# A streaming scale-and-add: rows regrouped from two halves into three contiguous blocks of HBM

## The chip, the core and the metric

One core of one Trainium2 chip at a time. The metric is the device time of one execution in microseconds (us). All runs quoted were in the fast state; the granted clock was 1.0 in every one. Ratios are the mean time of one kernel's fast runs over the mean of the other's in the same rounds, with a 95% interval, so they are not quite the ratios of the medians quoted beside them.

## The reference

```python
B, S, D = 1024, 16, 512          # bf16
def reference(x, y, gamma):      # x, y: B x S x D; gamma: D
    return x + gamma * y
```

That is 16384 rows of 1 KB in each of x, y and the output, 128 rows for each of 128 partitions: 33.6 MB to read, 16.8 MB to write, and one multiply and one add for each element.

## The kernel before

The kernel is written on bare queues and semaphores. SP issues the loads, ACT issues the small gamma load and the stores, VectorE multiplies and adds in place in `y_sb`. Four lists say everything about the order: `SP` and `ACT` list transfers as (tensor, first row, last row, place in the x buffer), `PIECES` cuts a partition's 128 rows into VectorE's pieces, `DVE` is VectorE's order of multiplies and adds.

```python
PIECES = [53, 11, 53, 11]
SP = [('y', 0, 64), ('x', 0, 64, 0), ('y', 64, 128), ('x', 64, 117, 0), ('x', 117, 128, 64)]
ACT = [('g',), ('s', 0, 64), ('s', 64, 128)]
RELEASE = ('x', 64, 117, 0)
DVE = [('m', 0), ('m', 1), ('a', 0), ('a', 1), ('m', 2), ('m', 3), ('a', 2), ('a', 3)]
...
xv = xf.rearrange("(p n) d -> p n d", p=P)       # partition p owns rows 128p .. 128p+127
y_sb = nc.alloc_sbuf_tensor("y_sb", [P, rows, D], dt).ap()
x_sb = nc.alloc_sbuf_tensor("x_sb", [P, x_rows, D], dt).ap()   # x_rows = 75: reused
...
            if need > known:
                eng.wait_ge(s_add, need)         # an x load waits for the add that frees its place
...
    _take(s_load[RELEASE], 16, nc.tensor)        # stores are let go when this load has landed
    nc.tensor.sem_inc(s_go, 1)
```

Two rules matter here. The x buffer holds 75 of a partition's 128 rows of x, so the fourth load waits for the first add. The stores are held back until the 53-row load has landed (76.5 us; the first store is issued at 76.88), while the load of the last 11 rows is still under way (it lands at 80.0); the store's first packet starts at 79.01, 2.1 us after its issue.

## Time and profile before

| | before |
|---|---|
| time, median of 6 runs (lowest to highest) | 119.99 us (119.86 to 120.15) |
| span of the profiled execution | 118.6 us |
| VectorE busy | 70.0 us, 59% |
| HBM traffic over the span | 424 GB/s |
| loads, stores | 5 (and gamma), 2 |
| VectorE passes over rows | 8 |

The prediction below shows the lines and reads them. In short: a transfer's line gives its issue and its time to landing; the landings of 64 rows follow each other every 19.3 to 19.4 us (433 to 434 GB/s), and VectorE waits for them. Where a transfer waits for VectorE, it is still issued before the engines run out of work. Besides the page, the trace has a record for every DMA packet (start, duration, bytes) and for each of the sixteen parts of a transfer's completion; a landing is the last of these parts. A packet is one partition's run of rows (65536 B for 64 rows), so each transfer of rows has 128 of them, and the packets follow each other in sixteen series with eight of each transfer: eight on an engine. Figures to a thousandth of a microsecond come from those records.

### The profile page before, as it was taken

How to read it: one execution, taken by the hardware profiler on the slowest of the kernel's cores; microseconds unless marked ns; L12 is line 12 of the kernel's file. 1: busy time of each engine (PE TensorE's matmuls, PEld its weight loads, DVE VectorE, ACT ScalarE, POOL GpSimd, SP SyncE). 2: the span in 40 equal slices, each digit the busy share in tenths (PEclk: the TensorE clock that was granted, in tenths of full speed). 3: DMA queues.
4: the chain of work that ended last, by engine and by line, in shares of the span. 5: the costliest groups of instructions: out<-in, count | busy, mean ns of one | idle time of the engine just before them, and what ended most of it. 6: DMA issues, size and time to landing. Idle time of an engine off the chain costs nothing. (4 is left out here: it accounts for less than half of the span.)

```text
span 118.6 us, 78 instructions
## 1 busy us (share of the span) xinstructions
PE 0.6 (0%) x1; PEld 0.1 (0%) x1; DVE 70.0 (59%) x10; POOL 0.2 (0%) x4
## 2 busy tenths in 40 slices
PE   0001000000000000000000000000000000000000
PEld 0000000000000000000000000000000000000000
DVE  0002000599999299999759999999999910000000
POOL 0000000000000000000000000000000000000000
DMA  9889888998899888998896969598899888988892
GB/s 354 354 376 685 354 354 354 597 464 354 354 398 663 354 354 354 663 398 354 354 586 293 586 293 567 220 639 354 354 575 486 354 354 376 685 354 354 354 619 88
DMA packets 1010, 50.33 MB, mean 424 GB/s; under 512 B 113, under 2 KB 114, under 8 KB 114
## 3 DMA queue, kind: packets, MB, share of 16 engines
q1 hardware_dynamic: 720, 33.55, 66.0%
q10 hardware_dynamic: 290, 16.78, 32.6%
HBM read 33.56 MB, written 16.78 MB: 424 GB/s over the span
## 5 line engine op out<-in xcount | busy, mean ns | idle before, releaser
L156 DVE TENSOR_TENSOR y_sb<-y_sb,gamma_sb 128x27136 bf16<-128x27136 bf16 (+1 forms) x4 | 34.6, 8688 | 12.7 <-DVEq L25 12.7
L165 DVE TENSOR_TENSOR y_sb<-x_sb,y_sb 128x27136 bf16<-128x27136 bf16 (+1 forms) x4 | 34.6, 8688 | 2.3 <-DVEq L25 2.2
L132 DVE CAST gamma_sb<-gamma_ps 128x512 bf16<-128x512 f32 x1 | 0.7, 692 | 8.8 <-DVEq L25 8.8
L127 DVE MEMSET ones_row<- 1x128 bf16 x1 | 0.2, 165 | 1.5 <-PEq L41 1.5
L130 PE MATMUL gamma_ps<-gamma_row,ones_row 1*128 1x512 bf16 x1 | 0.6, 578 | 9.7 <-PEq L25 9.7
L130 PEld LDWEIGHTS gamma_ps<-gamma_row,ones_row 1*128 1x128 bf16 x1 | 0.1, 100 | 9.7 <-issue 9.7
L194 POOL MEMSET const-uint8-127<- 128x1 uint8 x1 | 0.1, 102 | 0.0
L194 POOL MEMSET const-bfloat16-1.0<- 128x1 bf16 x1 | 0.1, 101 | 0.0
L194 POOL MEMSET const-float32-0.0<- 128x1 f32 x1 | 0.1, 98 | 0.2 <-issue 0.2
L194 POOL MEMSET const-float32-1.0<- 128x1 f32 x1 | 0.1, 98 | 0.0
## 6 DMA issues: line engine op xcount, KB each, us to landing
x_sb<-in_x_dram SPq DMA_DIRECT2D x1, 6784.0 KB, 20.8
x_sb<-in_x_dram SPq DMA_DIRECT2D x1, 1408.0 KB, 23.9
y_sb<-in_y_dram SPq DMA_DIRECT2D x2, 40.2
out_dram<-y_sb ACTq DMA_DIRECT2D x2, 22.8
x_sb<-in_x_dram SPq DMA_DIRECT2D x1, 39.7
gamma_row<-in_gamma_dram ACTq DMA_DIRECT2D x1, 1.0 KB
```

Source lines behind the costliest of these rows:

```text
L127: nc.vector.memset(ones_row, 1.0).then_inc(s_ones, 1)
L130: nc.tensor.matmul(gamma_ps, ones_row, gamma_row, start=True, stop=True).then_inc(s_ps, 1)
L132: nc.vector.tensor_copy(out=gamma_sb, in_=gamma_ps).then_inc(s_dve, 1)
L156: nc.vector.tensor_tensor(out=yt, in0=yt, in1=g, op=MULT).then_inc(s_dve, 1)
L165: nc.vector.tensor_tensor(out=yt, in0=xt, in1=yt, op=ADD).then_inc(s_add, 1)
L194: nc = _bacc.Bacc("TRN2", target_bir_lowering=False, num_devices=1)
```

## The change

The rows are regrouped into three pieces of 58, 58 and 12 rows per partition, and each piece is one contiguous block of HBM: partitions are 58 KB apart in it instead of 128 KB (12 KB in the small piece). The intent is an address pitch that is no power of two, with bigger pieces for VectorE. It takes one load and one store more.

```diff
-PIECES = [53, 11, 53, 11]
-SP = [('y', 0, 64), ('x', 0, 64, 0), ('y', 64, 128), ('x', 64, 117, 0), ('x', 117, 128, 64)]
-ACT = [('g',), ('s', 0, 64), ('s', 64, 128)]
+PIECES = [58, 58, 12]
+SP = [('y', 0, 58), ('x', 0, 58, 0), ('y', 58, 116), ('y', 116, 128), ('x', 58, 116, 0), ('x', 116, 128, 58)]
+ACT = [('g',), ('s', 0, 58), ('s', 58, 116), ('s', 116, 128)]
-RELEASE = ('x', 64, 117, 0)
-DVE = [('m', 0), ('m', 1), ('a', 0), ('a', 1), ('m', 2), ('m', 3), ('a', 2), ('a', 3)]
+RELEASE = ('x', 58, 116, 0)
+DVE = [('m', 0), ('a', 0), ('m', 1), ('m', 2), ('a', 1), ('a', 2)]
...
-    xv = xf.rearrange("(p n) d -> p n d", p=P)     (yv and ov alike)
+    def at(v, a, b):
+        assert a in starts and b - a in PIECES
+        return v[a * P : b * P].rearrange("(p n) d -> p n d", p=P)
...
-  in_=xv[:, w[1] : w[2], :]
+  in_=at(xf, w[1], w[2])                           (y loads and stores alike)
```

More of the change, by code (lines that the diff above doesn't have):

```diff
@@ L51 @@
     dt = xf.dtype
-    xv = xf.rearrange("(p n) d -> p n d", p=P)
-    yv = yf.rearrange("(p n) d -> p n d", p=P)
-    ov = of.rearrange("(p n) d -> p n d", p=P)
+    def at(v, a, b):
+        assert a in starts and b - a in PIECES
+        return v[a * P : b * P].rearrange("(p n) d -> p n d", p=P)
     gamma_row = nc.alloc_sbuf_tensor("gamma_row", [1, D], dt).ap()
@@ L112, in ring @@
                 to = x_sb[:, w[3] : w[3] + w[2] - w[1], :]
-                i = eng.dma_start(out=to, in_=xv[:, w[1] : w[2], :]).then_inc(s_load[w], 16)
+                i = eng.dma_start(out=to, in_=at(xf, w[1], w[2])).then_inc(s_load[w], 16)
             elif kind == "y":
                 r = slice(w[1], w[2])
-                i = eng.dma_start(out=y_sb[:, r, :], in_=yv[:, r, :]).then_inc(s_load[w], 16)
+                i = eng.dma_start(out=y_sb[:, r, :], in_=at(yf, w[1], w[2])).then_inc(s_load[w], 16)
             else:
                 r = slice(w[1], w[2])
-                i = eng.dma_start(out=ov[:, r, :], in_=y_sb[:, r, :]).then_inc(s_out, 16)
+                i = eng.dma_start(out=at(of, w[1], w[2]), in_=y_sb[:, r, :]).then_inc(s_out, 16)
             if k < n_early:
```

## The prediction

> **What bounds the kernel now.** I read the page's busy shares and DMA totals first, to see which resource is full; then the views of single operands, for when each transfer was issued and landed; then the timeline of VectorE, to see which landing each of its instructions waits for.
>
> ```profile
> span 118.6 us, 78 instructions
> PE 0.6 (0%) x1; PEld 0.1 (0%) x1; DVE 70.0 (59%) x10; POOL 0.2 (0%) x4
> ...
> HBM read 33.56 MB, written 16.78 MB: 424 GB/s over the span
> ```
>
> VectorE is busy for 59% of the span, nothing else computes, and the transfers average 424 GB/s over the whole span, start and end included. The suspect is the DMA engines. The next lines are the issues of the x loads, the y loads and the stores, each with its times from issue to landing (smallest, median, largest).
>
> ```profile
> L113 SPq DMA_DIRECT2D x_sb<-in_x_dram x3: 328/328/443, 1.4 to 56.1; - x3
> DMA to landing us min/median/max: 20.8/23.9/39.7
> ...
> L116 SPq DMA_DIRECT2D y_sb<-in_y_dram x2: 372/408/445, 0.0 to 1.8; - x2
> DMA to landing us min/median/max: 21.8/40.2/58.7
> ...
> L119 ACTq DMA_DIRECT2D out_dram<-y_sb x2: 339/354/370, 76.9 to 95.4; - x2
> DMA to landing us min/median/max: 22.4/22.8/23.2
> ```
>
> Issue plus time to landing gives the landings: y rows 0-63 at 0.0 + 21.8 = 21.8; x rows 0-63 at 1.4 + 39.7 = 41.1; y rows 64-127 at 1.8 + 58.7 = 60.5; x rows 64-116 at 55.7 + 20.8 = 76.5; x rows 117-127 at 56.1 + 23.9 = 80.0; the stores at 76.9 + 22.4 = 99.3 and 95.4 + 23.2 = 118.6. The gaps between landings of 64 rows (8.389 MB) are 19.3, 19.4, 19.3 and 19.3 us, or 433 to 434 GB/s, and the 53 rows take 16.0 us. So from 2.5 us (21.8 less 19.3) to the end the engines never run dry. The chain that ends last is the transfers themselves; the chain of waits, which cannot follow a stream of transfers, names little.
>
> The completions of a load's sixteen parts are in the trace more finely than the page prints them: on one DMA engine 64 rows took 19.354 us (mean of two), 53 rows 16.040 and 11 rows 3.391. 64 against 53 gives 3.314 / 11 = 0.3013 us per row, 53 against 11 gives 12.649 / 42 = 0.3012. One row on one engine is 8 partitions of 1 KB, so 8192 B / 0.3012 us = 27.2 GB/s, times 16 engines 435 GB/s. What is left is a **fixed 0.078 us per load** (16.040 - 53 x 0.3012); a store's 19.292 us leaves 0.02 us. The span is then 1.98 (start, until the first engine moves data at full rate) + 384 x 0.3012 = 115.66 + 5 x 0.078 + 2 x 0.02 + 0.53 (spread of the sixteen engines and the last wait) = 118.6. It closes on the profile's span with nothing over.
>
> ```profile
> 21.94 17.29 DVE L156 TENSOR_TENSOR y_sb<-y_sb,gamma_sb 128x27136 bf16<-128x27136 bf16 x2 [10.79 <-DVEq L25]
> 41.39 17.29 DVE L165 TENSOR_TENSOR y_sb<-x_sb,y_sb 128x27136 bf16<-128x27136 bf16 x2 [2.16 <-DVEq L25]
> 55.71 0.81 SPq L113 DMA_DIRECT2D x_sb<-in_x_dram  x2
> 60.63 17.29 DVE L156 TENSOR_TENSOR y_sb<-y_sb,gamma_sb 128x27136 bf16<-128x27136 bf16 x2 [1.95 <-DVEq L25]
> 76.88 18.86 ACTq L119 DMA_DIRECT2D out_dram<-y_sb  x2
> 78.07 17.29 DVE L165 TENSOR_TENSOR y_sb<-x_sb,y_sb 128x27136 bf16<-128x27136 bf16 x2
> ```
>
> The columns are start, duration and operation, with the idle time before in brackets. VectorE matters in two places only. It must free the x buffer (add done, loads issued at 55.71) before the queue of loads is empty at 60.5: **4.8 us to spare**. It must end the last large add before the first store is through at 99.3: the second store is issued at 95.40, **3.9 us to spare**.
>
> [...] Here a partition's pitch is 128 KB[...]: loads and stores run at 435 GB/s. [...]
>
> **The change part by part.** The build keeps 128 partitions on the SBUF side and one contiguous run per partition (58 or 12 KB in place of 64, 53 or 11), so each transfer should still use sixteen engines. Bytes are the same.
>
> *The address pitch.* Partitions come 58 KB apart (12 KB in the small piece) rather than 128 KB[...]. The bulk is at 435 GB/s already[...]. The one slow place is the start: the first sixteen packets took 2.70 to 3.40 us, all others of 64 KB 2.42, some 0.7 us lost on average. [...]
>
> *The transfers.* Six loads for five, three stores for two: 0.078 + 0.02 = **+0.10 us**, all of it on the path.
>
> *VectorE.* Six passes for eight. 27136 elements take 14.292 us and 5632 take 3.084, so 0.5212 ns an element plus 0.149 us: 29696 elements take 15.63 us, 6144 take 3.35. The sum falls by 2 x 0.149 = 0.3 us, beside the transfers. It frees nothing.
>
> *The two margins.* I walk the new order with 17.55 us per 58-row load (58 x 0.3012 + 0.078) and 3.69 us per 12-row load. y0 lands at 1.98 + 17.55 + 0.47 (from the first engine's landing to the sixteenth's, 21.33 to 21.81 now) = 20.0, x0 at 37.5, y1 at 55.1, y2 at 58.8, x1 at 76.3, x2 at 80.0. Multiply 0 runs 20.1 to 35.8, add 0 from 37.8 (0.25 after its landing, as before) to 53.4, when the last two loads are issued; the queue holds work until 58.8, so **5.4 us** are spare. Multiplies 1 and 2 run from 55.2 to 74.2, before x1 lands. Store 0 is released at 76.7, 0.35 after that landing as now. Add 1 runs 76.9 to 92.5, store 1 is issued at 92.6, and store 0 is through at 80.0 + 17.5 = 97.5: **4.9 us** spare. Add 2 ends at 95.9, store 2 is issued then, store 1 is through at 115.0, store 2 at 118.6. Both margins grow; neither was used.
>
> *Sum.* Span 118.6 + 0.1 = 118.7. Time 119.93 + 0.10 = **120.0 us**.
>
> **The rivals.** (a) *The pitch matters at the start.* [...] the first packets are slow. Against it: every later batch, stores as well as loads, ran with the same pitch at full rate. It would make 119.3 to 119.7, still inside 2%. (b) *A wait takes over.* If loads issued at 53.4 or the store issued at 92.6 reached the engines late, the queue would run dry. In the profile the first store's packets started 2.1 us after its issue, while loads were still moving; with 5 us spare I need a delay more than twice as long before it costs anything. To lose 2% (2.4 us), over 7 us would be needed. (c) *Unaligned or shorter runs cost bandwidth.* Rows of 58 KB start at multiples of 1 KB only and no store of that shape is in the profile. For it: stores are untested. Against it: the 53-row load has a run of 54272 B and its packets took 2.00 us each, exactly in proportion. If the nine transfers lost 1% each it would be 121.1. (d) *VectorE binds*: no, it has some 48 us idle.
>
> **Range and chances.** The sum gives 120.0. A faster start would take away up to 0.7 us and I give that one chance in eight; small extra costs of the new store pattern might add up to 0.6. The runs before differ by 0.3 us among themselves. So 119.5 to 120.6. Faster by 2% means under 117.5, a span under 116.2, against 115.7 for the bytes alone[...]: next to excluded, 0.01. Slower by 2% needs a dry queue or an unseen store penalty, 0.02. Within 2%: 0.97.
>
> **What would show it right or wrong.** Right: landings of the loads near 20.0, 37.5, 55.1, 58.8, 76.3 and 80.0, the last two loads issued near 53.4, stores issued near 76.7, 92.6 and 95.9, landing near 97.5, 115.0 and 118.6, and packets of 59392 B at 2.19 us (2.418 x 58 / 64). Wrong: packets longer or shorter than that in proportion (pitch or alignment matters); first packets without the excess (rival a); a gap between packets before x1 or store 1 (rival b); a time under 119.5 or over 120.6.

Passages are cut from the prediction, at the marks: most of a paragraph on rates and pitches that no run here shows, a reading of why the first packets are slow, the address distance between engines (no packet record names a partition; it is cut from two expectations below as well), and words that take 435 GB/s for the most the engines can do. The last was not shown: the profile has this rate for loads of 64 and 53 rows and for stores, and nothing that sets it. So the chance of 0.01 for faster rests on my estimate that the bulk would keep its measured 0.3012 us a row. The "up to 0.7 us" of rival (a) is the excess of the first sixteen packets (mean 3.11 us against 2.42).

## The result

| | before | changed |
|---|---|---|
| time, median of 6 runs | 119.99 us | 120.16 us (120.06 to 120.38) |
| ratio | | 1.0017, interval 1.0003 to 1.003 |
| span of the profiled execution | 118.6 us | 118.8 us |

The change costs two thousandths, some 0.17 us by the medians: the same within 2%. These are the lines of the changed kernel's page that answer to the first ones of before:

```profile
span 118.8 us, 79 instructions
PE 0.6 (0%) x1; PEld 0.1 (0%) x1; DVE 69.9 (59%) x8; POOL 0.2 (0%) x4
...
HBM read 33.56 MB, written 16.78 MB: 424 GB/s over the span
```

Two VectorE instructions fewer, the same traffic, the same rate. The views of the x loads, the y loads and the stores, with issue times and then the time from issue to landing (smallest, median, largest):

```profile
L115 SPq DMA_DIRECT2D x_sb<-in_x_dram x3: 327/328/452, 1.4 to 53.9; - x3
DMA to landing us min/median/max: 22.9/26.2/36.2
...
L118 SPq DMA_DIRECT2D y_sb<-in_y_dram x3: 371/458/478, 0.0 to 2.3; - x3
DMA to landing us min/median/max: 20.2/53.4/56.6
...
L121 ACTq DMA_DIRECT2D out_dram<-y_sb x3: 338/339/369, 76.8 to 96.0; - x3
DMA to landing us min/median/max: 20.9/22.4/22.8
```

And the timeline (start, duration, operation, idle time before):

```profile
20.30 15.62 DVE L158 TENSOR_TENSOR y_sb<-y_sb,gamma_sb 128x29696 bf16<-128x29696 bf16 x1 [9.98 <-DVEq L25]
37.92 15.62 DVE L167 TENSOR_TENSOR y_sb<-x_sb,y_sb 128x29696 bf16<-128x29696 bf16 x1 [2.00 <-DVEq L25]
53.58 0.82 SPq L115 DMA_DIRECT2D x_sb<-in_x_dram  x2
55.36 18.89 DVE L158 TENSOR_TENSOR y_sb<-y_sb,gamma_sb 128x29696 bf16<-128x29696 bf16 x2 [1.81 <-DVEq L25]
76.81 19.56 ACTq L121 DMA_DIRECT2D out_dram<-y_sb  x3
77.10 18.89 DVE L167 TENSOR_TENSOR y_sb<-x_sb,y_sb 128x29696 bf16<-128x29696 bf16 x2 [2.85 <-DVEq L25]
```

Issue plus time to landing gives loads landed at 20.2, 37.7 (1.4 + 36.2, with the issue unrounded), 55.2, 58.9, 76.5 and 80.1 us, and stores at 97.7, 115.2 and 118.8. Every one is within 0.2 us of the walk in the prediction, and always on the late side.

Where do the 0.2 us of span come from? Take the last store's sixteen parts. The first of them landed at 118.056 us before and at 118.157 in the changed kernel, 0.10 us later: this would be the term for one more load and one more store. The last of the sixteen came 0.515 us after the first before and 0.649 after it now, another 0.13 us. (By the mean of the sixteen parts the last store came 0.14 us later, and 0.15 in the second profiles, so 0.10 us is the low end of what the profiles show.) That second part is the spread of the engines, which starts with the first load (0.474 and 0.642 us) and is carried through to the end. So the question for the experiments was twofold: is the 0.10 us really the price of the transfers, and is the spread the pitch, the piece size, or chance? And, since nothing else moved, are the margins that kept everything else off the path as wide as I had said?

### The profile page after: what moved, and what is told of

The parts are those of the page before. It is cut to its first block, busy times and chain, and to the rows that moved or that the text cites. A ratio compares the mean times of both kernels' runs of the same rounds, so it can differ in the third digit from the quotient of the medians.

```text
span 118.8 us, 79 instructions
## 1 busy us (share of the span) xinstructions
PE 0.6 (0%) x1; PEld 0.1 (0%) x1; DVE 69.9 (59%) x8; POOL 0.2 (0%) x4
## 5 line engine op out<-in xcount | busy, mean ns | idle before, releaser
L158 DVE TENSOR_TENSOR y_sb<-y_sb,gamma_sb 128x29696 bf16<-128x29696 bf16 (+1 forms) x3 | 34.5, 11533 | 11.8 <-DVEq L25 11.8
L167 DVE TENSOR_TENSOR y_sb<-x_sb,y_sb 128x29696 bf16<-128x29696 bf16 (+1 forms) x3 | 34.5, 11534 | 4.8 <-DVEq L25 4.8
## 6 DMA issues: line engine op xcount, KB each, us to landing
out_dram<-y_sb ACTq DMA_DIRECT2D x1, 1536.0 KB, 22.8
```

The costliest lines, as they stand in the source:

```text
L158: nc.vector.tensor_tensor(out=yt, in0=yt, in1=g, op=MULT).then_inc(s_dve, 1)
L167: nc.vector.tensor_tensor(out=yt, in0=xt, in1=yt, op=ADD).then_inc(s_add, 1)
```

## The experiments

The theory (T): the sixteen engines stream from start to end, so each transfer's fixed cost is paid in full and nothing else counts. Rivals: the pitch matters after all, at the start or in the bulk; the transfer cost is hidden and the 0.1 us is something else; VectorE is nearer to the path than it looks. Twelve runs were made, in four groups, each group with runs of the kernel before on the same chip. All were correct. Most diffs show added lines alone; "..." marks a cut.

### The two kernels once more

No edit. Expected of the changed kernel:

> The changed kernel unaltered, for the size of the noise and a second profile of its start. Theory T (two terms: 0.10 us for one more load and one more store, and a start in which the slowest of the sixteen DMA engines is 0.13 to 0.17 us later): 120.1 to 120.2 against about 120.0, ratio 1.001 to 1.002, and in the profile the first load's sixteen parts land over 0.64 us again (19.52 to 20.16). Rival N (the start is noise and only the 0.10 us is real): ratio 1.0008, and the spread in this profile differs from 0.64 us, nearer the 0.47 of the kernel before.

and of the kernel before:

> The kernel before against itself. Both theories: ratio 1.000, interval holding 1. T: the first load's sixteen parts land over 0.47 us in this profile as well. N: the spread is another one, anywhere from 0.4 to 0.7 us.

The changed kernel measured 120.21 us against 119.99, ratio 1.0014 (1.0002 to 1.0026). The kernel before measured 120.10 against itself at 119.99, ratio 1.0005 (0.9992 to 1.0019): an offset of 0.05% means nothing here. In the second profiles the first of the last store's parts landed at 118.172 and 118.064 us, 0.11 us apart as in the first pair. The spread of the first load was 0.605 us (changed) and 0.545 (before, 0.474 in its first profile), so it moves by 0.07 us between two profiles of one kernel. **The 0.10 us repeats; the spread is partly chance.**

### Half of the change each

`pieces_only` keeps the lists of the changed kernel and goes back to the old addresses:

```diff
     def at(v, a, b):
-        assert a in starts and b - a in PIECES
-        return v[a * P : b * P].rearrange("(p n) d -> p n d", p=P)
+        return v.rearrange("(p n) d -> p n d", p=P)[:, a:b, :]
```

> Half of the change: the pieces, loads and stores of the changed kernel, but at the old addresses (partitions 128 KB apart[...]). If the number of transfers is all (N): 120.1, ratio 1.0008, like the changed kernel. If the pitch makes the late start (T, pitch form): first load lands over 0.47 us and the ratio is 1.0008, while the changed kernel shows 0.64 us and 1.0017. If the 58-row first packet makes it (T, size form): 0.64 us and 1.0017.

It measured 120.13 us, ratio 1.0011 (0.9999 to 1.0024), beside 1.0014 for the whole change in the same rounds. The first part of its last store landed at 118.175 us, like the changed kernel's 118.157 and 118.172. Its view of the x loads is that of the changed kernel within 0.1 us:

```profile
L114 SPq DMA_DIRECT2D x_sb<-in_x_dram x3: 328/328/443, 1.4 to 53.8; - x3
DMA to landing us min/median/max: 23.0/26.3/36.1
```

So what cost there is comes with the pieces, and the 58 KB pitch buys and costs nothing that shows. The engines' spread was 0.514 us in the first load, near the 0.47 of the theory's pitch form, but 0.736 in the last store, the largest of the three kernels although it has the old pitch. Over all profiles with first loads of 58 or 64 rows, the first load's spread lay between 0.47 and 0.65 us with partitions 128 KB apart and between 0.52 and 0.71 at 58 KB; by size, between 0.51 and 0.71 us with 58 rows and between 0.43 and 0.71 with 64. The ranges overlap, and two profiles of one kernel (`pitch_only` and its repeat, below) have 0.43 and 0.71: neither pitch nor size is shown to make the spread.

`pitch_only` keeps the lists of the kernel before and lays the rows out as two contiguous blocks of 64 (partitions 64 KB apart):

```diff
+    def at(v, a, b):
+        k = a // 64
+        assert b <= 64 * k + 64
+        block = v[64 * k * P : (64 * k + 64) * P].rearrange("(p n) d -> p n d", p=P)
+        return block[:, a - 64 * k : b - 64 * k, :]
```

> The other half: the transfers and VectorE passes of the kernel before, but its rows laid out as two contiguous blocks of 64 rows (partitions 64 KB apart[...]). N: ratio 1.000, 119.95 to 120.05. T, pitch form: first load lands over about 0.64 us and the ratio is about 1.001. If a smaller pitch helped at the start: under 0.47 us and a ratio below 1.

This was a surprise: 120.45 us, ratio 1.0036 (1.0023 to 1.0049), slower than the change although it has no transfer more than before. Its x loads:

```profile
L117 SPq DMA_DIRECT2D x_sb<-in_x_dram x3: 328/328/440, 1.4 to 56.0; - x3
DMA to landing us min/median/max: 21.1/24.2/39.7
```

Before, the view read 20.8, 23.9 and 39.7: the load of 64 rows is as it was, the two late loads take 0.3 us more. By the first of its sixteen parts the 53-row load took 16.360 us instead of 16.040, and its packets took up to 2.208 us where 2.004 is the rule. I ran it again:

> The layout of two 64-row blocks once more, unaltered. If its 0.45 us is a property of these addresses: ratio 1.003 to 1.004 again, and the 53-row x load again takes some 16.3 us per engine with packets over 2.05 us. If it was chance: ratio within 1.001 and 16.04 us.

Again slower: 120.38 us, ratio 1.0040 (1.0024 to 1.0056), the 53-row load 16.192 us, packets up to 2.17 us. Its profiled run was the fastest of the six in both cases, so the slower runs may hold more of this. **With these transfers this layout cost some 0.4 us twice; the layout of the change cost nothing that shows.**

### Is it a 53-row run out of each 64 KB?

Both kernels cut every 64-row load into 53 and 11 rows, so eight loads and two stores; one has the 64-row blocks, one the old addresses.

```diff
+SP = [('y', 0, 53), ('y', 53, 64), ('x', 0, 53, 0), ('x', 53, 64, 53), ('y', 64, 117), ('y', 117, 128), ('x', 64, 117, 0), ('x', 117, 128, 64)]
```

> The layout of pitch_only (two contiguous blocks of 64 rows, partitions 64 KB apart) with every 64-row load cut into 53 and 11 rows: eight loads, two stores. In pitch_only one 53-row load took 16.36 us per engine where the kernel before needs 16.04, while its 64-row loads ran at full speed. Theory P (a 53 KB run out of each 64 KB loses about 0.3 us per load): all four 53-row loads take some 16.3 us; the time is 120.0 + 3 more loads x 0.08 + 4 x 0.32 = about 121.5. Rival Q (the loss belongs to that one place, the load issued late behind the y load): only the third of the four, or none, is slow: 120.2 to 120.6.

> The same eight loads and two stores at the addresses of the kernel before (partitions 128 KB apart). Both P and Q: 53-row loads of 16.04 us, so 120.0 + 3 x 0.08 = 120.2. If 53-row loads are slow here too, the pitch is not the cause.

They measured 120.39 us (ratio 1.0036, 1.0021 to 1.0051) and 120.20 us (ratio 1.0021, 1.0006 to 1.0036). With the 64-row blocks the 53-row loads took 16.047, 16.035 and 16.035 us (the very first holds the start-up): none lost 0.3 us. So the run length at that pitch is not the cause by itself (theory P falls). Nor is it that one late load: away from the first sixteen packets, packets more than 2% over the usual 2.004 us began between 59.7 and 70.1 us in `pitch_only` (49 of them), between 63.7 and 72.1 us in its repeat (29), and between 3.8 and 11.7 us, in the first load, in the kernel with eight loads (9). At the old addresses no 53-row packet was that slow, but `pieces_only` had 11 slow 58-row packets between 28.0 and 52.5 us, so such stretches are not confined to one layout. What makes them stays open. The old addresses came out at 120.2 as expected for three more loads; the intervals of the two kernels overlap.

### Many transfers

The kernel before with 16 loads of 13, 14 or 16 rows and the one of 11, and stores of 16 rows: 17 loads for 5, 8 stores for 2.

```diff
+SP = (
+    [('y', r, r + 16) for r in range(0, 64, 16)]
+    + [('x', r, r + 16, r) for r in range(0, 64, 16)]
+    + [('y', r, r + 16) for r in range(64, 128, 16)]
+    + [('x', 64, 77, 0), ('x', 77, 90, 13), ('x', 90, 103, 26), ('x', 103, 117, 39), ('x', 117, 128, 64)]
+)
+ACT = [('g',)] + [('s', r, r + 16) for r in range(0, 128, 16)]
+RELEASE = ('x', 103, 117, 39)
```

> The kernel before with its loads and stores cut in four: 17 loads for 5 and 8 stores for 2, all else the same. Theory T (0.078 us per load and 0.02 per store, on the path because the engines never idle): 12 x 0.078 + 6 x 0.02 = +1.06, 121.05 us. Rival H (the cost of a transfer is hidden beside the next one, and the 0.1 us of the changed kernel is something else): 119.9 to 120.2.

It measured 120.90 us against 119.96, ratio 1.0075 (1.0060 to 1.0090): **+0.9 us where +1.06 was expected and nothing if hidden.** By the landings a 16-row load took 4.894 us on an engine; 16 times 0.3012 is 4.819, so 0.075 us would be the load's own; a 16-row store took 4.838, so 0.02. The first part of the last store came 1.01 us later than before (119.063 against 118.056), and the spread was smaller, 0.338 instead of 0.515 us, which gives back 0.18. So added transfers cost time, and rival H falls.

The packet records correct the size of the terms. Each transfer leaves a record of 4 bytes on each engine after its last packet. From one such record to the next an undisturbed transfer takes 19.319 us for 64 rows, 17.512 for 58, 16.006 for 53, 4.862 for 16 and 3.356 for 11, loads and stores alike. That is 0.3012 us a row and **0.043 us a transfer**. The landings follow these records by 0.35 to 0.52 us in the profiles of before, the changed kernel and `many`, and this lag drifts along the kernel, so differences of landings made loads look dearer (0.078) and stores cheaper (0.02) than they are. In `many` the stores and the first five loads keep to 4.862 us; later 16-row loads take 4.88 to 4.90, with packets of up to 0.619 us where 0.611 is the rule. So 18 x 0.043 = 0.77 us is the price of the transfers, and another 0.4 us or so is slower loads, of which the cause is not shown; 0.1 us is gained at the start. That the sum came so near to the expected 1.06 is partly luck. Every transfer here has eight packets on each engine, so no run separates a price per transfer from a price per packet.

### How wide are the margins?

These kernels add needless VectorE passes over a spare tile ahead of the first add of the changed kernel, which postpones the issue of the last two x loads (five passes took 6.72 us, their waits included, two 2.60). The lead of a load, below, is the time from its issue to the moment when the first engine has ended its last packet of the load before:

```diff
+EXTRA = 5        # 2 and 1 in the other two
...
+            if c == 0:
+                for _ in range(EXTRA):
+                    _take(s_dve, open_mults, nc.vector)
+                    g4 = gamma_sb[:, None, :].to_broadcast([P, 4, D])
+                    nc.vector.tensor_tensor(out=spare, in0=g4, in1=g4, op=MULT).then_inc(s_dve, 1)
+                    open_mults = 1
```

> The changed kernel with five needless VectorE passes (2048 elements each, by the slope 1.22 us, with waits some 1.37) ahead of the first add, so that the last two x loads are issued about 6.8 us later, at 60.4 rather than 53.6. The engines run out of loads at 58.4 to 58.9. Theory T with a start-up of 1.0 us from issue to first packet (as at the kernel's start): a gap of about 60.4 + 1.0 - 58.6 = 2.8, so 123.0. With a start-up of 2.1 us (as the first store shows): 124.1. If VectorE's work were on the path in itself: 120.2 + 6.8 = 127.0.

It measured 124.78 us (124.00 to 124.88), ratio 1.038. Neither form of the estimate was high enough. Windows of its profile (length, busy us of PE, PEld, DVE and POOL, clock, DMA share, GB/s) show the queue running dry:

```profile
56.00:58.00 2.00, 0.00 (x0) 0.00 (x0) 2.00 (x1) 0.00 (x0) 1.00 0.96 412
58.00:60.00 2.00, 0.00 (x0) 0.00 (x0) 2.00 (x1) 0.00 (x0) 1.00 0.00 0
60.00:61.20 1.20, 0.00 (x0) 0.00 (x0) 1.20 (x2) 0.00 (x0) 1.00 0.00 0
61.20:64.00 2.80, 0.00 (x0) 0.00 (x0) 2.80 (x1) 0.00 (x0) 1.00 1.03 339
```

No packet starts between 58.0 and 61.2 us. The load is issued at 60.34, its first packet starts at 61.30, so this restart took 0.95 us (at the start of both kernels the first packet came 1.0 us after the issue); then the sixteen first packets take 2.74 to 3.24 us, on average 0.71 us more than the 2.19 of all others. This is the same excess as at the very start of both kernels (0.69 and 0.67 us in the two profiles of before, 0.76 and 0.74 in those of the changed kernel). **The slow first packets came where the engines started from an empty queue, with partitions 128 KB apart and 58 KB apart**: here in the middle of the kernel, at 58 KB. The load as a whole took 21.495 us from the landing before it instead of 17.549, so 3.95 us were lost there, and the engines' spread, 0.52 us in the first load, was 1.19 by the end: it rose from 0.59 to 1.14 in the 12-row load, in which one packet took 1.08 us instead of 0.46.

> The changed kernel with two needless VectorE passes ahead of the first add: the last two x loads are issued 2.75 us later, at 56.3, still 2.1 us before the engines run out at 58.4. Theory T (five passes cost 3.9 us because a restart from an empty queue needs about 1.0 us to the first packet and about 0.7 us more for the first reads; nothing is lost while the new load is there in time): 120.2, the same as the changed kernel, and no gap between packets. Rival (VectorE's delay costs in proportion): 120.2 + 4.6 x 2/5 = 122.0.

A miss: 121.96 us (121.35 to 122.48), ratio 1.018 (1.0156 to 1.0203, which leaves open whether it is beyond 2%), some 1.8 us above the changed kernel in the first group. Its x loads and stores:

```profile
56.27 0.80 SPq L117 DMA_DIRECT2D x_sb<-in_x_dram  x2
...
L117 SPq DMA_DIRECT2D x_sb<-in_x_dram x3: 327/328/432, 1.4 to 56.6; - x3
DMA to landing us min/median/max: 20.2/24.7/36.2
...
L123 ACTq DMA_DIRECT2D out_dram<-y_sb x3: 338/339/371, 76.8 to 96.0; - x3
DMA to landing us min/median/max: 22.1/23.6/24.0
```

The load is issued at 56.27 and the first engine needs it at 57.86, when its last packet of y ends. There is no gap between packets, but the sixteen first packets take 2.19 to 2.68 us where 2.192 is the rule. The 58-row load then lands at 76.4, as without the delay; the 12-row load behind it lands on fifteen engines by 80.18 and on the sixteenth at 81.30, after three of its packets took 0.64, 0.76 and 1.20 us instead of 0.46. That one engine is a microsecond late for the rest, and the stores take 1.2 us longer to land (22.1, 23.6 and 24.0 after 20.9, 22.4 and 22.8). The profiled run was the fastest of the four, so the others lost more, in ways no profile shows. Why a single engine falls back some 20 us after the late issue I cannot say. The three packets ran from 77.9 to 80.5 us, just after the first store's issue at 76.80. In `delay5` the slow 12-row packet began at 82.8, after the store's issue at 80.74, and in the kernel before one packet of that load, begun at 78.1, took 0.62 us instead of 0.42. The late load itself cost 0.15 us on the mean of the engines. So the late issue brings the loss, by four runs of four, but the profile shows most of it where the stores start.

> The changed kernel with one needless VectorE pass ahead of the first add: the last two x loads are issued 1.37 us later, at 54.9, some 3.4 us before the engines run out. Two passes (2.1 us left) cost 1.8 us against an expectation of none. Theory M (a load must be with the engines some 2 to 3 us before its turn, and there is a threshold): 120.2, ratio 1.001 to 1.002, no packet of the late x load over 2.25 us, the sixteen landings of the last x load within 0.7 us. Rival R (every bit of delay costs, as the engines then fall out of step and the slowest sets the end): 120.6 to 121.3, one or two engines landing the last x load over 0.7 us after the others.

120.15 us, ratio 1.0005 (0.9992 to 1.0017): nothing lost. The load is issued at 55.01, 2.8 us before the first engine needs it at 57.84:

```profile
55.01 0.80 SPq L117 DMA_DIRECT2D x_sb<-in_x_dram  x2
```

All its first packets took 2.192 us, and the last load's sixteen parts landed within 0.689 us. So in this kernel a lead of 2.8 us is enough and one of 1.6 us is not. The kernel before has 3.9 us (issue at 55.71, first packet of that load at 59.645), the changed kernel 4.3 us (53.58 and 57.87).

### A try for something better

One load fewer than before: the x buffer is freed by a single 64-row add, the last x load is one of 64 rows, and the stores are let go by VectorE when the second big multiply is done.

```diff
+PIECES = [64, 53, 11]
+SP = [('y', 0, 64), ('x', 0, 64, 0), ('y', 64, 128), ('x', 64, 128, 0)]
+ACT = [('g',), ('s', 0, 64), ('s', 64, 117), ('s', 117, 128)]
+RELEASE = None
+DVE = [('m', 0), ('a', 0), ('m', 1), ('go',), ('m', 2), ('a', 1), ('a', 2)]
...
```

> A try for something better than both, at the old addresses: four loads of 64 rows and three stores, the x buffer freed in one pass, so one load fewer than before. The last x load is then issued at about 58.4, some 1.3 us before the first engine is empty at 59.7. Theory T (0.078 us per load, 0.02 per store, start-up 1.0 us): 119.99 - 0.08 + 0.02 = 119.9, no gap. If the start-up doesn't fit in 1.3 us: a gap before the last x load, and 120.3 to 121.5.

123.55 us, ratio 1.032 (1.0279 to 1.0364): clearly slower, and beyond both forms of the expectation. The profiled run, 124.79 us, was the slowest of the six.

```profile
58.72 0.33 SPq L113 DMA_DIRECT2D x_sb<-in_x_dram  x1
...
75.26 30.68 ACTq L119 DMA_DIRECT2D out_dram<-y_sb  x3
88.28 17.29 DVE L163 TENSOR_TENSOR y_sb<-x_sb,y_sb 128x27136 bf16<-128x27136 bf16 x2 [9.95 <-DVEq L25]
```

The load is issued 1.0 us before the first engine needs it (59.77), its first packets take up to 3.4 us, and VectorE waits 9.95 us for it. The early release of the stores may add to this: from 77 us on, after the first store's issue at 75.26, the last packets of the load take up to 4.3 us. The store's own packets start later, at 80.4 us and after, as each engine ends its last packet of that batch. The two causes were not separated, and no run tests alone what the small last load of both kernels is worth.

## Why the prediction was right

**What binds.** Right. `many` pays for each added transfer (0.043 us by the packet records), `delay1` postpones the last two loads by 1.4 us at no cost (ratio 1.0005), and `delay5` shows what it looks like when the engines do stop (no packet starts between 58.0 and 61.2 us). That the prediction's sum "closes with nothing over" proves less than it sounds: start, loads and stores are differences of successive landings, so they add up by construction; the terms themselves were tested by `many`, which corrects their size. On the one core used here loads and stores ran at 435 GB/s (0.3012 us a row on an engine); no run shows what sets this rate.

**The pitch.** Right for this change: `pieces_only` at the old addresses is as slow as the whole change (1.0011 and 1.0014), and packets of 59392 B took 2.192 us where 2.19 was worked out. Rival (a), a gain at the start, fell: the first packets kept their excess (0.76 us after 0.69), which a restart in the middle of `delay5` shows too (0.71). The reason given against it, that one sees from the bulk that the pitch is harmless, does not carry over to other layouts, as `pitch_only` shows (ratio 1.0036). Rival (c), a penalty for runs of 58 KB, fell with the packets too: those of the stores took 2.192 us like those of the loads.

**The transfers.** +0.10 us predicted; +0.10 and +0.11 us in the two pairs of profiles at the first of the sixteen parts. The time rose by 0.17 us (medians), and the rest goes with the wider spread of the engines (0.13 and 0.08 us wider in the two pairs). The sum was near, its terms were not: a load and a store cost 0.043 us each, 0.09 us together, where I had 0.078 and 0.02 from differences of landings. With before differing by 0.05% from itself, that remainder is not established as an effect of the change.

**VectorE.** The passes of 29696 and 6144 elements took 15.625 and 3.351 us, as worked out, and the gain stayed beside the transfers.

**The margins.** The times of issue were right to 0.2 us (53.58, 76.81, 92.76 and 96.03), but the margins were overstated. I counted 5.4 us up to the landing of the load before; what counts is when the first engine ends its last packet of it and needs the next, which leaves 4.3 (3.9 before instead of 4.8). For the second store it is 3.8 instead of 4.9 (2.9 before instead of 3.9). The 2.1 us that I read as a store's start-up measure no start-up: in the profile of before each engine's first store packet began within 0.01 us of the end of its last load packet, so the store was waiting for its turn. And I wrote that losing 2% would take a delay of over 7 us: 2.7 us (`delay2`) cost 1.8% and 6.8 us cost 3.8%. The step that failed is the assumption that a load is in time as long as its start-up fits, 1.0 us by the start or 2.1 by the first store; in this kernel a lead of 1.6 us cost time and one of 2.8 us did not, though the last part of the late load landed on time (76.4 us), and the cause of the loss stays open. The change left more room than that, so this error did not reach the result.

## What to carry to other kernels

When the landings in a profile follow each other at a constant rate from start to end, try to sum the time as rows at that rate plus a cost per transfer plus the start and the end. In this kernel (0.3012 us a row, 0.043 us a transfer) it could be summed to about a tenth of a microsecond, and a change that left the bytes alone and the engines supplied moved the time by 0.17 us. Moving the data to other addresses has to be tried, not argued: of two tidy layouts one cost nothing that shows (58 KB, 1.0014 against 1.0011 at the old addresses) and one 0.4 us (64 KB, ratios 1.0036 and 1.0040). Count a margin in a stream of transfers from the issue of the next transfer to the end of the first engine's last packet of the present one, not to its landing; in this kernel that gave 4.3 us for a load where the landing gave 5.4, and 2.8 us of it were enough and 1.6 us were not (ratios 1.0005 and 1.018).
